# Two rates for a background conversion of weights, and twelve products of zeros early in an attention stage

## The chip, the cores and the metric

The kernel runs on one core of a Trainium2 chip. The metric is the device time of one execution in microseconds (us). The text calls the engines PE (matrix products), DVE (vector), ACT (activations), POOL and SP, as the profile does.

## What is computed

The reference is a chain of three layers on 1792 tokens (4 batches of 448). The first is attention with sigmoid weights, 12 heads of 64:

```
scores = scale * np.matmul(q, k.transpose(0, 1, 3, 2)) - np.log(S)
attn = 1.0 / (1.0 + np.exp(-scores))
return np.matmul(attn, v)
```

The second layer gives each token to one of 8 experts. Token-expert pairs are taken in falling order of their gate product, and an expert takes 224 tokens at most; each expert is two products with a ReLU between them. The third is a feed-forward layer with a leaky ReLU (2048 hidden units), whose weights `w_in` and `w_out` come in as 64-bit floating-point numbers.

## The kernel before

**Attention.** Four heads make a unit, `n`; there are 3 units in a batch and 12 in all. A unit has 7 steps (`STEPS_OF`), so there are 84 steps, numbered `i` here, 21 to a batch. For each step `scores(i)` (L368, L371) issues four products of 64x64 and one sigmoid on ACT, which does the step's whole tile; `values(i - 2)` (L391) follows two steps later (`LATE = 2`) and adds into PSUM tiles `pav`, of which there are 3. Twice per unit DVE adds two such tiles into `xT` (L397, L400), which sets a `pav` tile free. The scores' PSUM tiles `psc` are two.

**Loads.** Six loads of `qkv` go out at the start on SP's queue: five pieces of unit 0 and then all of unit 1. The load of unit n+2 is issued during unit n.

**Warming products.** `keep_warm` (L351) issues products of a tile of zeros, 128x128 times 128x384 in bf16, into a PSUM tile that nobody reads. Fourteen of them stand ahead of the first step.

**The conversion.** `narrow` (from L404 on) is a generator that turns the 64-bit words of `w_in` (16 parts) and of 13 of the 16 blocks of `w_out` into 32-bit numbers. A part is a tile of 128x768. Its operations, in their order:

- POOL issues the load of the words (L416, L418); four tiles of words exist, and the load for part i+4 is issued after part i.
- ACT takes the absolute value of the high words (L423) for even parts; DVE does this (L437) for odd parts.
- DVE clamps (L441), DVE shifts (L443), ACT scales the low words into a tile `cl` (L445), of which there are two; DVE merges the sign (L447).
- POOL adds the two (L458), and for `w_out` it issues a store of the part before (L428).

Its first `yield` stands after the first four loads. Then an odd part has four `yield`s (after L437, L441, L445, L447) and an even part three. The add on POOL (L458) comes with the next call.

**The order.** All engines work in program order. The loop over steps (L514 on) calls `scores(i)`, `aside(i)`, `values(i - 2)`, one piece of routing work if there is one, and `aside(i)` again. `aside` (from L500) adds `PACE` to an account and calls `next(back)` once for each whole unit on it. It begins with step 9. `back` is the conversion.

**Routing work.** After a batch's last value its gate products, the choice of an expert, the comparisons of all tokens (DVE, L202 to L208, more of them with every batch) and the counts (PE, L215, L219) are put on the list `todo`, which the next batch's steps take one by one; the copies of `x` to memory (`turns`, L331 on PE, L334 on ACT) go ahead of them. The last batch's pieces come after the loop. Behind them, `for _ in back: pass` calls whatever is left of the conversion. Then L897 runs, and `settle` closes expert 0: a chain from the counts over PE (L573), DVE (L578 on), POOL (`by`, L606) and a gather to the first expert's tokens.

Of the kernel before, what the change touches and what calls it, by code (L numbers as in the profile page):

```python
# [24 lines left out]
def attention_experts_ffn(  # L25
# [55 lines left out]
    ps_m = att.enter_context(tc.tile_pool(name="ps_m", bufs=1, space=PSUM))  # L81
# [8 lines left out]
    def load(n, a=0, z=3 * QV):  # L90
        if a == 0:
            qkv_sb[n] = ld.tile([P, 3 * QV], F32, name="qkv")
        nc.sync.dma_start(qkv_sb[n][:, a:z], qkv[n // NQ, n % NQ, :, a:z])
# [225 lines left out]
    def turns(b):  # L319


        x = xT[b]

        def turn(t0):
            w = min(P, S - t0)
            xt = aw.tile([P, DM], F32, name="xt", bufs=3)
            p = ps_s.tile([P, 2, 512], F32, name="psc")
            for i in range(HP):
                for s in range(w // D):
                    for z in range(2):  # L330
                        nc.tensor.matmul(p[halves[s], z, i * D:(i + 1) * D],  # L331
                                             x[halves[z], i, t0 + s * D:t0 + (s + 1) * D],
                                             ident[halves[z], halves[z]], start=True, stop=True)
            nc.scalar.copy(xt[:w].rearrange("p (i z d) -> p z i d", z=2, d=D),  # L334
                           p[:w, :, :HP * D].rearrange("p z (i d) -> p z i d", d=D))
            nc.sync.dma_start(x_dram[b * S + t0:b * S + t0 + w, :], xt[:w])

        return [lambda t0=t0: turn(t0) for t0 in range(0, S, P)]
# [7 lines left out]
    def keep_warm(ps, tag, n):  # L346
        if not n:
            return
        p = ps.tile([P, 512], F32, name=tag)[:, :3 * P]
        for _ in range(n):  # L350
            nc.tensor.matmul(p, idle[:, :P], idle, start=True, stop=True)  # L351
# [4 lines left out]
    STEPS_OF = [(0, c) for c in range(KC)] + [(None, KC)] + [(1, c) for c in range(KC)]  # L356
    steps = [(n, r, c) for n in range(B * NQ) for r, c in STEPS_OF]
    LATE = 2
    halves = [slice(0, D), slice(D, P)]

    def scores(i):
        n, r, c = steps[i]
        p = ps_s.tile([P, 2, 512], F32, name="psc")
        for s in range(2):
            for z in range(2):
                a = c * P + z * D if r is not None else KC * P
                w = r if r is not None else z
                nc.tensor.matmul(p[halves[z], s, :S], k_of(n, w, a, a + D)[halves[s]], q_of(n, w)[halves[s]],  # L368
                                 start=True, stop=True)
        AT[i] = aw.tile([P, 2, S], F32, name="at", bufs=LATE + 2)  # L370
        nc.scalar.activation(AT[i], p[:, :, :S], AF.Sigmoid, bias=bias, scale=1.0 / math.sqrt(D))  # L371

    def values(i):
        n, r, c = steps[i]
        b, m = divmod(n, NQ)
        if (r, c) == (0, 0):
            if m == 0:
                xT[b] = aw.tile([P, HP, S], F32, name="xT")
            PV[0, 1] = ps_v.tile([P, 512], F32, name="pav")
            PV[0, 0] = ps_v.tile([P, 512], F32, name="pav")  # L380
        if r is None:
            PV[1, 1] = ps_v.tile([P, 512], F32, name="pav")
        if (r, c) == (1, 0):
            PV[1, 0] = ps_v.tile([P, 512], F32, name="pav")
        a = AT.pop(i)
        for z in range(2):
            w = r if r is not None else z
            first = (w, z) == (1, 1) and r is None or (w, z) != (1, 1) and c == 0
            last = (w, z) == (0, 0) and r is None or (w, z) != (0, 0) and c == KC - 1
            for s in range(2):  # L390
                nc.tensor.matmul(PV[w, z][halves[s], :S], v_of(n, c, 2 * w + s if r is not None else s)[halves[z]],  # L391
                                 a[halves[z], s, :], start=first, stop=last)
        x = xT[b]
        if (r, c) == (0, KC - 1):
            nc.scalar.copy(x[:, 2 * m, :], PV[0, 1][:, :S])
        elif r is None:
            nc.vector.tensor_tensor(x[:, 2 * m, :], x[:, 2 * m, :], PV[0, 0][:, :S], op=OP.add)  # L397
        elif (r, c) == (1, KC - 1):
            nc.scalar.copy(x[:, 2 * m + 1, :], PV[1, 1][:, :S])  # L399
            nc.vector.tensor_tensor(x[:, 2 * m + 1, :], x[:, 2 * m + 1, :], PV[1, 0][:, :S], op=OP.add)  # L400
# [97 lines left out]
    owed = [0.0]  # L498

    def aside(i):  # L500

        if i > 8:
            owed[0] += PACE
            while owed[0] >= 1:
                next(back, None)
                owed[0] -= 1

    nc.sync.dma_start(wg[:, :, :E], w_gate.rearrange("(c p) e -> p c e", p=P))
    nc.sync.dma_start(al, alpha.rearrange("(c p) -> p c", p=P))
    PACE = 0.68  # L510
    keep_warm(ps_m, "pm", 14)
    NS = len(steps)
    BS = NQ * len(STEPS_OF)
    for i in range(NS + LATE):  # L514
        if i < NS:
            scores(i)
            n, at_step = divmod(i, len(STEPS_OF))

            if LATE < at_step <= LATE + 3 and n + 2 < B * NQ:
                a = (at_step - LATE - 1) * QV  # L520
                load(n + 2, a, a + QV)
        aside(i)
        k = i - LATE
        if k == NS - 1:
            final = after_batch(B - 1)
            final.pop(0)()
        if k >= 0:
            values(k)
        for turns_left in (rows_todo, todo):
            if turns_left:  # L530
                turns_left.pop(0)()
                break
        aside(i)
        if k >= 0 and k % BS == BS - 1:
            b = k // BS
            todo += after_batch(b) if b + 1 < B else final
            (rows_todo if b + 2 < B else rows_end).extend(turns(b))
# [792 lines left out]
```

## Time and profile before

| | us |
|---|---|
| median of 3 runs | 1005.82 |
| lowest and highest of these | 1005.04, 1006.96 |
| the profiled execution's own time | 1013.2 |
| its span, first to last instruction | 1011.3 |

The profile's span has 96% of busy PE. The attention stage with the routing of the first expert takes the first fifth (about 0 to 208 us); experts and feed-forward layers take the rest. A row of the timeline gives the start and the duration in us, then engine, line, operation, tile written and tiles read, shapes, how many are merged into the row, and in brackets the idle time of the engine before it and what ended it.

### The profile page before, as it was taken

What the parts mean: (1) busy time and instruction counts of PE and PEld (TensorE: products, weight loads), DVE (VectorE), ACT (ScalarE), POOL (GpSimd) and SP (SyncE); (2) the same over time, 40 slices, a digit from 0 to 9 for tenths busy, and PEclk for the clock granted to TensorE, in tenths of its full rate; (3) what the DMA queues carried; (4) which work ended last, traced back from release to release, by engine and by line L of the source; (5) the groups of instructions that cost most, each with busy time, mean ns of one, the idle gap of its engine ahead of it and who ended that gap; (6) DMA issues with size and microseconds to landing.
All of it is one profiled execution on the core that took longest, in us unless ns stands there. A gap on an engine that the chain in (4) does not pass through costs nothing.

```text
span 1011.3 us, 17392 instructions
## 1 busy us (share of the span) xinstructions
PE 968.4 (96%) x6793; PEld 792.3 (78%) x6793; DVE 665.9 (66%) x1297; ACT 523.8 (52%) x875; POOL 217.4 (21%) x300
## 2 busy tenths in 40 slices
PE   7999999889789999999999999999999999999995
PEld 3444433569788878899988898999999999999994
DVE  1669899797667797477777745777643477644342
ACT  3989777311454343466643344765343466644442
POOL 1435465122720000711000060300120111000001
PEclk8999999999989999999999999999999999999998
DMA  8687884465531121257403131861321167311101
GB/s 289 217 307 247 305 322 147 158 242 194 179 133 36 54 100 48 71 181 253 140 32 110 47 104 48 255 236 35 109 91 63 43 188 256 111 47 48 63 32 54
DMA packets 41523, 141.44 MB, mean 140 GB/s; under 512 B 9250, under 2 KB 9842, under 8 KB 41314
## 3 DMA queue, kind: packets, MB, share of 16 engines
q1 hardware_dynamic: 26210, 72.40, 21.2%
q0 software_dynamic: 15232, 67.95, 20.0%
q8 instruction: 53, 0.87, 0.4%
q14 instruction: 28, 0.23, 0.1%
HBM read 122.86 MB, written 17.46 MB: 139 GB/s over the span
## 4 chain that ended last, share of the span: by engine, by line
PE 70%; DVE 11%; ACT 7%; DMA 5%; issue 4%; POOL 2%; SPq 0%; DVEq 0%; ACTq 0%; POOLq 0%
PE pa L1162 18%; PE pz L1142 18%; PE pa L1060 15%; PE psc L368 4%; PE pav L391 4%; PE pa L954 2%; PE pa L934 2%; ACT si L985 2%; DMA wm<-in_w_dram 2%; PE pa L1142 1%; DVE t L1063 1%; POOL pk L762 1%; DMA qkv<-in_qkv_dram 1%; PE pa L1201 1%; DMA wo_dram<-ct 1%
## 5 line engine op out<-in xcount | busy, mean ns | idle before, releaser
L1162 PE MATMUL pa<-gx,so 128*128 128x448 f32 x1152 | 251.8, 368 | 0.3 <-issue 0.3
L1142 PE MATMUL pz<-y,si 128*128 128x448 f32 x1080 | 230.3, 367 | 1.2 <-ACT R L183 1.2
L1162 PEld LDWEIGHTS pa<-gx,so 128*128 128x128 f32 x1152 | 213.9, 188 | 19.8 <-issue 2.2
L1142 PEld LDWEIGHTS pz<-y,si 128*128 128x128 f32 x1080 | 202.1, 188 | 18.5 <-ACT R L183 1.7
L1145 ACT ACTIVATE gx<-pz 128x448 f32<-128x448 f32 x60 | 32.7, 545 | 244.6 <-PE pz L1142 244.6
L1147 DVE SCALAR_TENSOR_TENSOR gx<-gx,nalpha 128x448 f32<-128x448 f32 x64 | 43.7, 683 | 143.9 <-ACT gx L1146 130.2
L1100 POOL DMA_DIRECT2D wo<-wo_dram x64 | 35.5, 556 | 447.4 <-DVE so L1107 218.0
L1060 PE MATMUL pa<-y,si 128*128 128x448 f32 x336 | 112.8, 388 | 1.1 <-DVE y L1023 1.1
L1060 PE MATMUL pa<-gx,si 128*128 128x448 f32 x336 | 108.6, 380 | 0.0
L990 DVE TENSOR_TENSOR so<-wm,si 128x768 fp32r<-128x768 f32 (+1 forms) x98 | 103.9, 1063 | 2.1 <-PE pa L1162 1.1
L368 PE MATMUL psc<-qkv 64*64 64x448 f32 x672 | 100.2, 560 | 4.2 <-DMA qkv<-in_qkv_dram 2.9
L371 ACT ACTIVATE at<-psc,bias 128x896 f32<-128x896 f32 x84 | 84.7, 1019 | 37.4 <-PE psc L368 37.1
L391 PE MATMUL pav<-at,qkv 64*64 64x448 f32 x672 | 102.2, 553 | 1.4 <-ACT xT L399 1.0
L985 ACT CAST si<-wm 128x768 fp32r<-128x768 f32 (+1 forms) x98 | 89.7, 920 | 1.5 <-DMA wm<-in_w_dram 1.5
L1060 PE MATMUL pa<-y,so 128*128 128x224 f32 x336 | 82.9, 274 | 7.5 <-DVE so L990 7.4
L1060 PE MATMUL pa<-gx,so 128*128 128x224 f32 x336 | 83.3, 268 | 0.3
L1060 PEld LDWEIGHTS pa<-y,so 128*128 128x128 f32 x336 | 65.8, 196 | 11.9 <-DVE so L990 9.5
L1063 DVE TENSOR_TENSOR t<-pa,t 128x224 f32<-128x224 f32 x98 | 38.3, 391 | 53.1 <-ACT t L1062 47.7
L1060 PEld LDWEIGHTS pa<-y,si 128*128 128x128 f32 x336 | 63.1, 195 | 5.0 <-ACT si L985 1.3
L391 PEld LDWEIGHTS pav<-at,qkv 64*64 64x64 f32 x672 | 34.8, 136 | 41.0 <-issue 31.1
L1151 DVE TENSOR_TENSOR gx<-gx 128x448 fp32r<-128x448 f32 x64 | 40.0, 625 | 40.6 <-ACT gx L1150 40.6
L1060 PEld LDWEIGHTS pa<-gx,so 128*128 128x128 f32 x336 | 64.5, 192 | 2.7 <-DVE so L990 1.7
(215 smaller groups left out, 1438.6 us busy)
## 6 DMA issues: line engine op xcount, KB each, us to landing
wm<-in_w_dram SPq DMA_DIRECT2D x64, 384.0 KB, 4.0
wm<-in_w_dram SPq DMA_DIRECT2D x48, 512.0 KB, 4.9
wo<-wo_dram POOLq DMA_DIRECT2D x64, 384.0 KB
qkv<-in_qkv_dram SPq DMA_DIRECT2D x31, 448.0 KB, 5.3
words<-in_w_in_dram POOLq DMA_DIRECT2D x16, 768.0 KB
words<-in_w_out_dram POOLq DMA_DIRECT2D x13, 768.0 KB
wo_dram<-ct POOLq DMA_DIRECT2D x13, 384.0 KB
x_dram<-xt SPq DMA_DIRECT2D x12, 384.0 KB, 4.9
```

Source lines behind the costliest of these rows:

```text
L368: nc.tensor.matmul(p[halves[z], s, :S], k_of(n, w, a, a + D)[halves[s]], q_of(n, w)[halves[s]], start=True, stop=True)
L371: nc.scalar.activation(AT[i], p[:, :, :S], AF.Sigmoid, bias=bias, scale=1.0 / math.sqrt(D))
L391: nc.tensor.matmul(PV[w, z][halves[s], :S], v_of(n, c, 2 * w + s if r is not None else s)[halves[z]], a[halves[z], s, :], start=first, sto ...
L985: nc.scalar.copy(hi, w)
L990: nc.vector.tensor_tensor(lo, w, hi.bitcast(F32), op=OP.subtract)
L1060: nc.tensor.matmul(o, a[:, c, :], y, start=(c == 0 and s == 0), stop=(c == k - 1 and s == 1))
L1063: nc.vector.tensor_tensor(t, p[:, :CAP], t, op=OP.add)
L1100: nc.gpsimd.dma_start(RW[f], wo_dram[f * P:(f + 1) * P, :])
L1142: nc.tensor.matmul(z[:, :n], a[:, c, :], m[:, c, :n], start=(c == 0 and s == 0), stop=(c == HP - 1 and s == 2))
L1147: nc.vector.scalar_tensor_tensor(t, dn, nalpha[:, f:f + 1], up, op0=OP.mult, op1=OP.add)
L1151: nc.vector.tensor_tensor(gl, t, gh.bitcast(F32), op=OP.subtract)
L1162: nc.tensor.matmul(acc[d][:, :n], a[:, d * P:(d + 1) * P], m, start=(f == 0 and s == 0), stop=(f == NF - 1 and s == 2))
```

## The change

The account of `aside` grows by 0.95 per call up to step `BS + LATE` = 23 and by 0.57 from step 24 on, where it grew by 0.68 throughout. Twelve products of zeros are issued ahead of `scores(7)`, the first of the second unit (the second four heads).

```diff
     def aside(i):
 
         if i > 8:
-            owed[0] += PACE
+            owed[0] += EARLY if i <= BS + LATE else PACE
             while owed[0] >= 1:
                 next(back, None)
                 owed[0] -= 1
...
-    PACE = 0.68
+
+    EARLY, PACE = 0.95, 0.57
     keep_warm(ps_m, "pm", 14)
     NS = len(steps)
     BS = NQ * len(STEPS_OF)
     for i in range(NS + LATE):
+        if i == len(STEPS_OF):
+            keep_warm(ps_m, "pm", 12)
         if i < NS:
             scores(i)
```

## Rows read from the trace of the kernel before

**Rows 1.** Page, part 1: busy us of each engine over the whole span.
```profile
PE 968.4 (96%) x6793; PEld 792.3 (78%) x6793; DVE 665.9 (66%) x1297; ACT 523.8 (52%) x875; POOL 217.4 (21%) x300
```
**Rows 2.** Windows: stretch, busy us of PE, PEld, DVE, ACT, POOL, granted clock, DMA share, GB/s.
```profile
28.00:52.00 24.00, 23.14 (x273) 10.81 (x269) 17.94 (x22) 21.49 (x26) 11.60 (x10) 1.00 0.67 241
52.00:63.00 11.00, 10.64 (x230) 6.01 (x224) 5.11 (x8) 9.58 (x12) 4.10 (x5) 1.00 0.86 309
63.00:97.00 34.00, 34.00 (x429) 14.63 (x419) 31.16 (x47) 29.21 (x36) 16.71 (x14) 1.00 0.75 262
97.00:131.00 34.00, 33.42 (x413) 14.32 (x409) 28.35 (x48) 27.67 (x36) 16.46 (x14) 1.00 0.84 303
131.00:181.00 50.00, 46.04 (x536) 17.30 (x531) 45.62 (x67) 35.52 (x44) 28.25 (x26) 0.97 0.60 217
```
**Rows 3.** Timeline of ACT: the sigmoids of steps 7, 10 and 24 (one each step).
```profile
23.95 1.01 ACT L371 ACTIVATE at<-psc,bias 128x896 f32<-128x896 f32 x1 [0.50 <-PE psc L368]
...
28.76 1.01 ACT L371 ACTIVATE at<-psc,bias 128x896 f32<-128x896 f32 x1 [0.80 <-PE psc L368]
...
52.88 1.01 ACT L371 ACTIVATE at<-psc,bias 128x896 f32<-128x896 f32 x1
```
**Rows 4.** The start: PE's and SP's timelines, landing times of qkv (0:60), a window.
```profile
13.88 1.01 PE L368 MATMUL psc<-qkv 64*64 64x448 f32 x3 [2.90 <-DMA qkv<-in_qkv_dram]
...
0.77 2.77 SPq L93 DMA_DIRECT2D qkv<-in_qkv_dram  x6
...
DMA to landing us min/median/max: 2.6/6.6/15.5
...
10.00:20.00 10.00, 7.10 (x42) 2.54 (x41) 0.00 (x0) 2.59 (x3) 0.00 (x0) 0.66 0.98 331
```
**Rows 5.** Timeline of PE: products of zeros between the steps of expert 0's routing.
```profile
196.31 1.63 PE L351 MATMUL pa<-idle 128*128 128x384 bf16 x9
...
198.45 2.11 PE L351 MATMUL pa<-idle 128*128 128x384 bf16 x12
```
**Rows 6.** The conversion: timelines of POOL and DVE; groups by form, 28 to 52 us.
```profile
84.86 2.02 POOL L458 TENSOR_TENSOR w_in_sb<-ct,cl 128x768 int32<-128x768 int32 x1 [2.03 <-DVE ct L447]
...
84.62 0.56 DVE L437 TENSOR_SCALAR ct<-words 128x768 int32<-128x768 int32 x1
85.22 2.08 DVE L441 TENSOR_SCALAR ct<-ct 128x768 f32<-128x768 f32 x1
...
88.34 0.95 DVE L447 SCALAR_TENSOR_TENSOR ct<-words,ct 128x768 int32<-128x768 int32 x1
89.21 0.55 DVE L441 TENSOR_SCALAR ct<-ct 128x768 f32<-128x768 f32 x1
...
93.31 1.94 DVE L437 TENSOR_SCALAR ct<-words 128x768 int32<-128x768 int32 x1
...
L441 DVE TENSOR_SCALAR ct<-ct 128x768 f32<-128x768 f32 x5 | 4.8, 966 | 4.4 <-ACT ct L423 4.4
...
L437 DVE TENSOR_SCALAR ct<-words 128x768 int32<-128x768 int32 x3 | 4.0, 1322 | 0.0
```
**Rows 7.** The last batch: chain of waits, timelines of DVE and PE.
```profile
137.80 9.41 DMA wo_dram<-ct
...
147.33 1.06 DVE L437 TENSOR_SCALAR ct<-words 128x768 int32<-128x768 int32 x1 [1.31 <-DMA wo_dram<-ct]
...
148.81 0.35 PE L215 MATMUL pm<-g,OH 112*32 112x448 bf16 x1 [2.25 <-DVE g L208]
```
**Rows 8.** Behind the loop: DVE, POOL; and a small DVE operation beside a POOL add.
```profile
196.66 0.29 DVE L578 TENSOR_TENSOR tmp<-pc,OH 112x128 f32<-112x128 f32 x1 [1.85 <-PE pc L573]
...
180.53 1.09 POOL L428 DMA_DIRECT2D wo_dram<-ct x2
...
140.05 1.82 POOL L458 TENSOR_TENSOR ct<-ct,cl 128x768 int32<-128x768 int32 x1 [1.01 <-ACT at L371]
...
140.27 1.65 DVE L173 TENSOR_TENSOR a<-PK,M 112x32 f32<-112x32 f32 x1
```

## The prediction

> **What bounds the kernel now.** I read the page's totals first, then windows over the attention stage, then the timelines of the engines there. PE is busy for 96% of the span [rows 1], so whatever delays PE in this stage arrives at the end; the experts behind it only move as a block. The windows [rows 2] show three regimes. From 28 to 52 us (steps 10 to 23) PE idles 0.86 us, ACT is at 21.49 of 24 and DVE has 6 us free. From 63 to 131 PE is the bound: 34.00 of 34, then 33.42 of 34, with DVE at 31.16 and 28.35 right beneath it. From 131 to 181 (the last batch) PE idles 3.96 us and the granted clock is 0.97, while DVE is at 45.62 of 50. There PE waits for DVE: 2.25 us for a comparison whose turn came late behind a conversion that itself had waited 1.31 us for a store that took 9.41 us [rows 7]. The change thus takes conversion from where DVE is late and puts it where DVE has room; the question is whether that room is enough.
>
> **What the paces do.** Two calls a step at 0.68 from step 9 on make 20 calls by step 23, 73 by step 62 and the whole 102 in the loop (1 fetch, 15 even parts of 3, 14 odd of 4). At 0.95 and 0.57 it is 28 by step 23, 72 by step 62 and 99 by step 85. So steps 10 to 23 take 8 more calls, steps 24 to 62 nine fewer (44 for 53), the last batch about three fewer, and three calls are left for behind the loop.
>
> **A call's price on DVE.** Seven calls are an even and an odd part: two times L441, L443 and L447 and one L437, at 0.56, 0.56, 0.96 and 0.56 us [rows 6], 4.7 us. While POOL adds, though, a DVE operation takes as long as the add: L441 2.08 us instead of 0.55 beside POOL's 2.02 [rows 6]. A full DVE pays 1.5 us per part, 7.7 us per seven calls, 1.1 us a call. The stretch from 84.62 to 93.31 holds exactly seven calls and two sums of L397 and L400: 8.7 us, so 0.5 is left for each sum.
>
> The Trainium skill (SBUF — State Buffer, Who interferes with whom) says that DVE and POOL share a port pair that is locked for a whole instruction, and whoever comes second blocks fully. The trace agrees with 2.08 us beside 0.55.
>
> **Part A, the zeros.** Twelve products take (2.11 - 1.63) / 3 = 0.16 us each [rows 5], together 1.9 us of PE at full clock. They stand ahead of step 7, whose sigmoid came at 23.95 in an unbroken cadence [rows 3]. Unit 1's load was the sixth issued, by 3.54 us, and no load took over 15.5 us [rows 4]: it was there by 19.0, so step 7 waited for nothing. Steps 7 to 9 have no conversion beside them, so nothing else hides the zeros: +1.9 (0 if step 7 does wait).
>
> **Part B, the first batch.** Calls 2 to 28 put seven whole parts and most of an eighth on DVE: 27 x 4.7 / 7 = 18 us, plus seven POOL adds at 1.5 (10.5), plus four sums of some 0.5 (2): 30.5 us. The room is from 30.6 us (the first absolute value on ACT behind step 10's sigmoid at 28.76) to step 24's scores, a us ahead of 52.88 [rows 3]: some 21.5 us. DVE is then 9 us late. PE feels that in two places: ACT's L445 has two tiles `cl` and waits for the POOL add of two parts earlier, and that wait holds the sigmoids behind it; and the sums free the `pav` tiles. Five calls lie between an add and the L445 that needs its tile, worth 5.5 us of DVE less the add's own 1.8; two steps between scores and values and three to four between a sum and its tile's next use cover 2 to 5 us more. So 9 us late is 1 to 5 us on PE. From below: the five adds in this stretch lengthened DVE by only 5 x 0.41 + 3 x 0.77 = 4.3 us [rows 6], 0.87 each; then DVE is 4.6 late, all of it covered, and what is left is ACT: 8 calls with 3 operations in seven, each at most the 1.01 us of a sigmoid, which is on a larger tile [rows 3], are up to 3.4 us against its 2.5 us of idle time [rows 2]; I put +0.5 there. I take +2.0 (0.5 to 5.5), nearer the lower row because the lengthening is seen in this very stretch. From 52 to 63 DVE has 5.9 us free and PE is held by the copies of x, so DVE's delay ends there. The words' loads move on too: 8 calls are 2.3 parts of 768 KB, in 24 us 75 GB/s on 241; the window of [rows 4] carried 331, so I cost this at nothing.
>
> **Part C, steps 28 to 62.** Nine calls fewer are 10 us less on DVE, but PE has only 0.58 us of idle time to give back [rows 2]: -0.5 (0 to -0.6).
>
> **Part D, the last batch.** The ceiling is PE's idle 3.96 us and the clock, 0.03 x 50 = 1.5 us: -5.5. DVE arrives without the backlog of the second and third batch and does three calls fewer, 3.3 us; the store has 3.1 steps per part where it had 2.6, so its wait of 1.31 us goes, and with it the idle time ahead of the lower clock. DVE is then at 45.62 - 3.3 = 42.3 us beside PE's 50 - 5.5 = 44.5, near enough that some waits stay: -4.5 (-2.5 to -5.5).
>
> **Part E, behind the loop.** L458 of one part and the whole last part come after the comparisons. On DVE 0.56 + 0.56 + 0.96 = 2.1 us go ahead of L578, where DVE idles for 1.85 us [rows 8]: +0.2. Then POOL's add of 1.8 us meets the short operations of `settle`; one of 112x32 elements took 1.65 us beside such an add [rows 8]. POOL also issues two stores ahead of `by` and the gather, 1.09 us for two. Everything up to the first expert waits for this chain. Bounds: +0.2 (the add falls into a wait for PE) and +3.1 (0.2, 1.8 and 1.1 in full); I take +1.5.
>
> **Sum.** 1.9 + 2.0 - 0.5 - 4.5 + 1.5 = +0.4 us on the profiled execution's 1013.2. That execution is 7.4 us above the median of 1005.82; I carry the difference over: 1006.2. About 0.2% (2 us) is what a measurement of this kernel can tell from no change.
>
> **The rivals.**
> 1. *The room suffices.* DVE's lengthening stays at the 0.87 us of the old first batch, the backlog is gone from step 28 on, and the last batch reaches its ceiling: 1.9 + 0.5 - 0.6 - 5.5 + 0.2 = -3.5, 1002.3; lower where idle time that the modelled ends of PE's products hide comes back as well. For it: DVE's 6 us free. Against it: 27 calls ask for more than that.
> 2. *The zeros fill a wait.* If unit 1's load came after step 6, PE would idle there and its clock fall, as after the 2.90 us at 13.88: the stretch from 10 to 20 us was granted 0.66, part of it the lower of the two levels (1.2 GHz for 2.4) [rows 4], 3.4 of 10 us lost. Then A is not +1.9 but up to -3.4: 1000.9. Against it: the landing by 19.0. The Trainium skill (TensorE: Matmul & The Clock Gate, HAM oscillation — how this bites in real kernels) says that a PE left idle in waits for loads is throttled again and each burst starts cold, for which zeros would be the cure. By that rule the first wait is such a place and the trace agrees (0.66); the zeros stand behind it.
> 3. *The first batch becomes DVE's* (slower). Every add lengthens DVE by 1.5 us, and the two `cl` tiles pass the delay on to the sigmoids. A step then asks DVE for 1.9 x 1.1 + 0.15 = 2.2 us in the 1.7 that a step took there (24.1 us for 14 [rows 3]), so from step 18 on DVE is over 4 us late, and that decides it. Then B is 5.5, the last batch gives 2.5 and the tail costs 3.1: 1.9 + 5.5 - 2.5 + 3.1 = +8.0, 1013.8; with the tail at 1.5 it is +6.4. For it: the full lengthening in the row at 85.22. Against it: this stretch's mean of 0.87.
>
> By the lock rule of the SBUF page taken alone every add would block a full DVE, which is rival 3.
>
> **Chances.** Forecast 0.36 (0.28 within the bound, 0.03 faster, 0.05 slower), rival 1 0.30 (all faster), rival 2 0.07 (0.05 faster, 0.02 within), rival 3 0.27 (slower). Faster 0.38, same 0.30, slower 0.32. The forecast's own range is 1004 to 1008.5; the range over all, 1000 to 1011, leaves out the far ends of rivals 2 and 3.
>
> **What would show it.** A: twelve L351 near 23 us, step 7's sigmoid 1.9 later, with no wait for qkv. B: L441 or L437 near 2 us at most adds before step 24, waits of L445 for POOL, PE idle over 0.86 us there. C and D: PE idle in the last batch under 2 us, clock 1.00. E: L458 beside L578 to L596 and `settle` longer by 1 to 2 us. If PE shows no idle time before step 24, B is wrong; if the last batch still idles by 4 us, D is.

## The result and the profile after

The changed kernel takes **1014.58 us** (median of 4 runs, 1012.85 to 1021.71) where the kernel before took 1005.81 beside it: a ratio of 1.0102, with a 95% interval of 1.006 to 1.0143. That is 8.8 us slower, and above the range of the prediction. The profiled execution is the longest of the four, 1021.71 us with a span of 1019.8.

The engine totals hardly differ. First the page's totals of the changed kernel, which answer to [rows 1]:

```profile
PE 973.5 (95%) x6805; PEld 793.8 (78%) x6805; DVE 666.1 (65%) x1297; ACT 523.4 (51%) x875; POOL 221.7 (22%) x300
```

DVE's instructions are the same 1297, PE's are twelve more. So the time is in when things happen. The start of the same event in both profiled executions, stage by stage (the sigmoids are those of ACT's timeline, as in [rows 3]; the others are the first transposes of the last counts on PE, L573 of before, and the first products of experts and of the feed-forward layer):

| stretch | before, us | after, us | difference |
|---|---|---|---|
| sigmoid of step 6 to that of step 7 | 1.5 | 3.7 | +2.2 |
| steps 10 to 24 | 24.1 | 30.1 | +6.0 |
| steps 24 to 83 | 122.8 | 115.4 | -7.4 |
| step 83 to the transposes L573 | 20.1 | 27.0 | +6.9 |
| the transposes to `tmp` (L578) | 0.8 | 6.9 | +6.0 |
| `tmp` to the first product of expert 0 | 15.1 | 15.5 | +0.4 |
| that product to the feed-forward layer's first | 95.6 | 87.9 | -7.7 |
| from there to the end | 703.9 | 706.4 | +2.5 |

Step 83's sigmoid stands at 175.7 us before and at 176.1 after: within the loop, cost and gain cancel. The loss stands behind the loop. The last two rows are stages that the change does not touch; the row of 95.6 and 87.9 lies between 86.7 and 100.8 over all profiled executions below, so I judge the change by what comes ahead of it. The 95.6 also belongs to an execution of the kernel before that took 7.4 us more than its median. How late step 6 comes differs as well (19.2 to 22.8 us over the executions), so I compare stretches rather than positions.

The windows of the changed kernel, with the columns of [rows 2] (busy us of PE, PEld, DVE, ACT and POOL, granted clock, DMA share, GB/s), cut at its own stages:

```profile
30.00:61.00 31.00, 26.41 (x282) 10.21 (x278) 27.95 (x30) 25.50 (x32) 17.54 (x14) 0.97 0.68 237
...
133.00:176.00 43.00, 42.29 (x447) 16.52 (x441) 37.54 (x60) 34.84 (x43) 21.47 (x22) 1.00 0.70 252
176.00:203.00 27.00, 23.49 (x451) 14.97 (x443) 18.20 (x37) 10.60 (x16) 4.67 (x4) 0.75 0.40 148
203.00:225.50 22.50, 15.03 (x100) 9.73 (x99) 14.60 (x49) 3.33 (x8) 8.61 (x13) 0.85 0.41 133
```

In the first batch DVE is at 27.95 of 31 and PE idles for 4.6 us, where it idled for 0.86 [rows 2]. In the last batch PE idles for 0.71 us in 43 at full clock, where it was 3.96 in 50 at 0.97 [rows 2]. From 203 to 225.5 PE is idle for a third of the time.

**The zeros** stand where they were expected. ACT's sigmoids of steps 6 and 7 of the changed kernel, to hold against [rows 3]:

```profile
22.13 1.01 ACT L371 ACTIVATE at<-psc,bias 128x896 f32<-128x896 f32 x1 [0.49 <-PE psc L368]
25.87 1.01 ACT L371 ACTIVATE at<-psc,bias 128x896 f32<-128x896 f32 x1 [2.73 <-PE psc L368]
```

**The first batch.** The next rows are from the timelines of POOL, DVE, PE and ACT after, and the last two group DVE's operations by form from 30 to 60 us (busy us, mean ns of one):

```profile
34.84 2.01 POOL L458 TENSOR_TENSOR w_in_sb<-ct,cl 128x768 int32<-128x768 int32 x1 [30.68 <-DVE ct L447]
...
39.42 1.98 POOL L458 TENSOR_TENSOR w_in_sb<-ct,cl 128x768 int32<-128x768 int32 x1 [2.02 <-DVE ct L447]
...
35.19 2.08 DVE L441 TENSOR_SCALAR ct<-ct 128x768 f32<-128x768 f32 x1
...
39.77 2.05 DVE L443 TENSOR_SCALAR ct<-ct 128x768 int32<-128x768 int32 x1
...
43.73 1.65 DVE L441 TENSOR_SCALAR ct<-ct 128x768 f32<-128x768 f32 x1
...
47.47 2.06 DVE L443 TENSOR_SCALAR ct<-ct 128x768 int32<-128x768 int32 x1
...
55.19 2.06 DVE L443 TENSOR_SCALAR ct<-ct 128x768 int32<-128x768 int32 x1
...
58.16 0.61 DVE L400 TENSOR_TENSOR xT<-xT,pav 128x448 f32<-128x448 f32 x1
...
53.09 0.98 PE L368 MATMUL psc<-qkv 64*64 64x448 f32 x8 [1.47 <-ACT at L371]
...
58.83 0.34 PE L331 MATMUL psc<-ident,xT 64*64 64x64 f32 x8 [2.06 <-DVE xT L400]
...
44.99 0.94 ACT L445 ACTIVATE cl<-words 128x768 int32<-128x768 uint32 x1 [0.42 <-POOL w_in_sb L458]
...
51.23 0.90 ACT L423 ACTIVATE ct<-words 128x768 f32<-128x768 f32 x1 [1.14 <-DMA words<-in_w_in_dram]
...
L443 DVE TENSOR_SCALAR ct<-ct 128x768 int32<-128x768 int32 x7 | 8.4, 1200 | 0.2
L441 DVE TENSOR_SCALAR ct<-ct 128x768 f32<-128x768 f32 x7 | 7.6, 1086 | 3.1 <-ACT ct L423 3.1
```

Every add of POOL now finds DVE with something queued and lengthens one operation from 0.55 us to between 1.65 and 2.08; L441 and L443 have means of 1086 and 1200 ns where an undisturbed one takes 0.56 [rows 6]. DVE runs late, and PE feels it at 58.83: the copies of `x` (L331) wait 2.06 us for the sum of L400, which DVE reached only at 58.16.

The wait of 1.47 us at 53.09 comes from further back: ACT had stood 1.14 us for a load of words at 51.23, which POOL issues only after an add. That load is not the limit. In the eight profiled executions, this one and seven of the experiments, that have this first batch with full adds, PE idles 4.57 to 4.59 us between steps 10 and 24 and the stretch takes 30.0 to 30.2 us, also in those three in which ACT waits 0.12 us or less for words. What they share is DVE, busy for 27.95 of 31 us in the window above. After the pauses the clock was granted 0.68 from 58 to 61 us, where before had 1.00 [rows 2].

**Behind the loop.** Timelines of DVE and POOL after, answering to [rows 8], then what the view of the tile `ct` says from 198 us on (who waited for it, and its stores from issue to landing):

```profile
201.91 0.55 DVE L441 TENSOR_SCALAR ct<-ct 128x768 f32<-128x768 f32 x1
...
203.97 0.17 DVE L900 TENSOR_SCALAR nalpha<-al 128x16 f32<-128x16 f32 x1
209.97 0.29 DVE L581 TENSOR_TENSOR tmp<-pc,OH 112x128 f32<-112x128 f32 x1 [5.83 <-issue]
...
204.20 1.79 POOL L458 TENSOR_TENSOR ct<-ct,cl 128x768 int32<-128x768 int32 x1 [17.82 <-ACT cl L445]
205.95 1.09 POOL L428 DMA_DIRECT2D wo_dram<-ct  x2
...
  DVE tmp L581: 5.8, 1
...
DMA to landing us min/median/max: 2.6/2.9/3.2
```

`tmp`, the first operation of `settle` on DVE, reads `pc` and `OH` alone, and PE's transposes into `pc` start at 203.10; before, it followed them by 0.8 us, here by 6.9, at 209.97. The profile's "issue" names no releaser, but the second of the last two stores goes out at 206.5 and 3.2 us later it has landed: 209.7, 0.27 us ahead of `tmp`. Before, the wait there was 1.85 us for PE, and the last two stores had been issued at 180.53 [rows 8].

### The profile page after: what moved, and what is told of

The parts are those of the page before. It is cut to its first block, busy times and chain, and to the rows that moved or that the text cites. A ratio compares the mean times of both kernels' runs of the same rounds, so it can differ in the third digit from the quotient of the medians.

```text
span 1019.8 us, 17409 instructions
## 1 busy us (share of the span) xinstructions
PE 973.5 (95%) x6805; PEld 793.8 (78%) x6805; DVE 666.1 (65%) x1297; ACT 523.4 (51%) x875; POOL 221.7 (22%) x300
## 3 DMA queue, kind: packets, MB, share of 16 engines
q1 hardware_dynamic: 26210, 72.40, 21.5%
## 4 chain that ended last, share of the span: by engine, by line
PE 63%; DVE 15%; issue 6%; ACT 6%; DMA 5%; POOL 4%; SPq 0%; DVEq 0%; POOLq 0%; ACTq 0%
PE pa L1165 18%; PE pz L1145 18%; PE pa L1063 13%; POOL pk L765 3%; PE psc L368 3%; PE pav L391 3%; PE pa L937 2%; DMA wm<-in_w_dram 2%; DVE ct L443 1%; PE pa L1145 1%; ACT si L988 1%; DMA qkv<-in_qkv_dram 1%; DVE t L1066 1%; DVE g L208 1%; PE pa L1204 1%
## 5 line engine op out<-in xcount | busy, mean ns | idle before, releaser
L1150 DVE SCALAR_TENSOR_TENSOR gx<-gx,nalpha 128x448 f32<-128x448 f32 x64 | 43.7, 684 | 145.1 <-ACT gx L1149 145.1
L371 ACT ACTIVATE at<-psc,bias 128x896 f32<-128x896 f32 x84 | 84.4, 1012 | 36.6 <-PE psc L368 35.9
L368 PE MATMUL psc<-qkv 64*64 64x448 f32 x672 | 91.9, 561 | 5.8 <-DMA qkv<-in_qkv_dram 3.3
L391 PE MATMUL pav<-at,qkv 64*64 64x448 f32 x672 | 93.3, 548 | 0.9 <-ACT xT L399 0.8
L1063 PEld LDWEIGHTS pa<-gx,si 128*128 128x128 f32 x336 | 61.3, 189 | 4.4 <-DVE gx L1071 0.6
```

The costliest lines, as they stand in the source:

```text
L1063: nc.tensor.matmul(o, a[:, c, :], y, start=(c == 0 and s == 0), stop=(c == k - 1 and s == 1))
L1150: nc.vector.scalar_tensor_tensor(t, dn, nalpha[:, f:f + 1], up, op0=OP.mult, op1=OP.add)
```

## The experiments

Two accounts were to be told apart. **The tail**: the three calls left behind the loop cost most of the loss, because `settle` waits for the last stores. **The first batch**: its 6 us are the loss (rival 3 of the prediction), and the tail is small. The first four experiments shared one chip, on which before had a median of 1005.06 us (1001.78 to 1006.65). On the chips of the later ones before lay at 1013.48 and 1012.53, with runs up to 15 and 17 us apart, so there the stages of the profiles say more than the ratios.

**Without the zeros.** From the changed kernel:

```diff
-        if i == len(STEPS_OF):
-            keep_warm(ps_m, "pm", 12)
```

> The changed kernel without its twelve products of zeros. Theory 1 (the three calls left behind the loop cost most: settle's first vector operation waits for the last stores): about 1.9 us under the changed kernel, 1012.7 against 1014.6, since the zeros are plain PE time ahead of step 7. Theory 2 (the denser first batch costs most): the same 1.9. If the zeros save a clock drop, this run is no faster or slower than the changed kernel.

Measured: 1014.31 us, 1.0097 (1.007 to 1.0125). The paces carry the loss, with the zeros or without. The 1.9 us that both accounts expected back do not show in the median, which is 0.3 us lower. Steps 10 to 24 take 30.2 us, and `tmp` comes 6.9 us after the transposes, as in the changed kernel.

**All calls done in the loop.** From the changed kernel, zeros kept:

```diff
-    EARLY, PACE = 0.95, 0.57
+    EARLY, PACE = 0.95, 0.61
```

> The changed kernel with 0.61 for 0.57, so that all 102 calls and the last add come inside the loop, as before the change; 0.95 and the zeros stay. Theory 1: 6 to 9 us under the changed kernel (1006 to 1008.5), and settle's first vector operation starts within 0.5 us of the transposes it reads. Theory 2: no change, 1013 to 1015, as the first batch is the same.

Measured: 1009.63 us, 1.0046 (1.003 to 1.0062), 5.0 us less than the changed kernel's median where I had expected 6 to 9. The first batch is as long as there (30.2 us), so it is not what made the difference. In the timelines of DVE and POOL of this kernel the last stores leave at 185.20, ahead of the end, and `tmp` waits for PE again, as before:

```profile
201.35 0.29 DVE L581 TENSOR_TENSOR tmp<-pc,OH 112x128 f32<-112x128 f32 x1 [1.85 <-PE pc L576]
...
185.20 1.09 POOL L428 DMA_DIRECT2D wo_dram<-ct  x2
```

**The tail alone.** From the kernel before, one pace that also leaves three calls behind the loop:

```diff
-    PACE = 0.68
+    PACE = 0.645
```

> The kernel before with one pace of 0.645 for 0.68: 99 calls in the loop, three left, no dense first batch, no zeros. Theory 1: 5 to 8 us over the kernel before (1011 to 1014), with a wait of about 6 us at settle's first vector operation. Theory 2: within 1 us of the kernel before, 1005 to 1007.

Measured: 1013.22 us, 1.0076 (1.0046 to 1.0106), 8.2 us above before's median. Steps 10 to 24 keep their length (24.2 us) and steps 10 to 83 even take 141.9 where before took 146.9. All that and more is lost behind the loop: 47.8 us from step 83 to the first expert's product, where before took 36.0. Timelines of DVE and POOL there, then PE's wait for DVE behind step 83 and a window (columns as above), and last that wait in the kernel before:

```profile
195.46 0.17 DVE L897 TENSOR_SCALAR nalpha<-al 128x16 f32<-128x16 f32 x1
201.47 0.29 DVE L578 TENSOR_TENSOR tmp<-pc,OH 112x128 f32<-112x128 f32 x1 [5.84 <-issue]
...
197.43 1.09 POOL L428 DMA_DIRECT2D wo_dram<-ct  x2
...
175.09 0.77 PE L256 MATMUL pm<-ident,l 128*112 128x128 f32 x2 [3.59 <-DVE l L254]
...
175.00:180.00 5.00, 4.91 (x106) 3.59 (x106) 1.53 (x3) 2.08 (x3) 0.17 (x1) 0.50 0.19 73
```

```profile
178.86 0.47 PE L256 MATMUL pm<-ident,l 128*112 128x128 f32 x2 [0.92 <-DVE l L254]
```

The second store goes out at 198.0 and lands 3.2 us later, at 201.2; `tmp` follows at 201.47. Of the 11.8 us lost, 6.0 are this wait. Another 5.2 lie between step 83 and the transposes: PE waits 3.59 us for DVE where it had waited 0.92, and then runs at half the clock.

This is the run that decides: a kernel without the busy first batch and without zeros has the loss, and one with both but without the calls behind the loop has half of it, most of which the zeros cost by themselves (next run).

**The zeros alone.** From the kernel before:

```diff
+        if i == len(STEPS_OF):
+            keep_warm(ps_m, "pm", 12)
```

> The kernel before with the twelve products of zeros ahead of step 7 and nothing else. Both theories: 1.9 us over the kernel before, 1007.7, with step 7's sigmoid 1.9 us later. If something later hides them: 1005.8.

Measured: 1008.57 us, 1.0036 (1.0025 to 1.0048), 3.5 us slower. The sigmoids of steps 6 and 7 are 3.7 us apart, as after, so 2.2 us are in place; where the other 1.3 us arise this profile does not settle (steps 10 to 83 take 1.6 us less than in the profile of before, and the way from there to the first expert 1.0 more). The costs do not add up: without the zeros the changed kernel lost as much as with them.

**Stores ahead of the last part.** From the changed kernel: the last two stores are issued with the one before them and from its tile, which leaves two blocks of `w_out` with another block's values; the calls and the last add stay.

```diff
-                _, f, h = parts[i]
-                nc.gpsimd.dma_start(wo_dram[...], outs.pop(i).bitcast(F32))
+                t = outs.pop(i).bitcast(F32)
+                if i < len(parts) - 2:
+                    for _, f, h in parts[i:] if i == len(parts) - 3 else parts[i:i + 1]:
+                        nc.gpsimd.dma_start(wo_dram[...], t)
```

> The changed kernel, with the last two stores of converted weights issued together with the one before them and from its tile (two blocks of 128 rows of w_out are wrong), so that no store follows the last add; the add and the vector operations stay where they are. Theory 1: settle's first vector operation starts at the end of the last add, about 3.8 us earlier: 1010 to 1011.5. If the wait is for the add and not for the stores: no gain, 1014.

Measured: 1017.0 us, 1.0015 (0.9966 to 1.0064), with runs from 1008.76 to 1025.22, so the stage has to tell. The transposes and `tmp` are 2.9 us apart where the changed kernel has 6.9. Timelines of DVE and POOL:

```profile
198.98 0.29 DVE L583 TENSOR_TENSOR tmp<-pc,OH 112x128 f32<-112x128 f32 x1 [1.89 <-POOL ct L460]
...
197.14 1.80 POOL L460 TENSOR_TENSOR ct<-ct,cl 128x768 int32<-128x768 int32 x1 [12.56 <-ACT cl L447]
```

With the stores out of the way `tmp` waits for the next thing in line, the end of POOL's add on `ct` at 198.94, although it does not read `ct`. So here the wait is for the last user of `ct`, a store or an add, and not for the stores as such. In the code `att.close()` stands between L897 and `settle`; that the tiles behind it take over the space, and so wait for all that still uses the old ones, is the reading that fits, and no run tested it by itself.

**The rest of the conversion ahead of the last batch's pieces.** From the changed kernel, and again from the kernel before with 0.645 in place of 0.68:

```diff
+    for _ in back:
+        pass
     for _ in range(2):
         rows_end.pop(0)()
```

> The changed kernel, with the three calls that are left drained right behind the loop, ahead of the last batch's routing pieces instead of behind them. Theory 1 (settle's first vector operation waits for the last stores): that wait of 5.8 us falls to what it was before the change, 1.85 us behind the transposes; the calls' 2 to 4 us of vector time move ahead of the comparisons; 3 to 6 us under the changed kernel, 1009 to 1012. Theory 2 (the first batch): no gain, 1013 to 1016.

> The kernel before with one pace of 0.645 and the three calls left drained right behind the loop. In the run with 0.645 alone step 83 came 6.5 us earlier than before and the wait behind the loop took 6. Theory 1: the wait goes, the gain in the loop stays in part: 1001 to 1005, at or under the kernel before. Theory 2 (the conversion must be early to be cheap): 1006 to 1009.

> The changed kernel with the three calls that are left drained right behind the loop, measured again because the first session's times scattered. Theory 1: 0 to 6 us under the changed kernel of this call; from step 83 to the first expert's product some 43 us, without a wait between the transposes and settle's first vector operation. Theory 2: as the changed kernel.

Measured: 1026.97 (three runs above 1026 and one at 1011.33), 1023.46 (1.0102, 1.0032 to 1.0172) and, the first again, 1027.19 (1.0132, 1.0067 to 1.0197). The wait ahead of `tmp` is gone in all three (0.8 us after the transposes), but the pieces wait behind the calls instead: step 83 to the transposes takes 28.2, 30.7 and 27.5 us where before needs 20.1, so from step 83 to the first expert it is 43.7, 46.7 and 43.5. The clock was granted half (1.2 GHz for 2.4) for some 10 us in that stretch or more each time, from 185.3 to 195.5 in the first. That this costs the gain is a miss of mine. On top, the stage from the first expert to the feed-forward layer took 100.2 to 100.8 us in these three. ACT's timeline of the first shows two pauses in it:

```profile
282.09 0.34 ACT L1067 COPY t<-pa 128x224 f32<-128x224 f32 x1 [4.95 <-remote]
...
290.62 0.34 ACT L1067 COPY t<-pa 128x224 f32<-128x224 f32 x1 [6.62 <-remote]
```

"remote" is a releaser that the profile cannot name. No edit touches that stage, and the last experiment has the same 100.7 us without this edit. Eleven of the twelve runs of these kernels lie above 1020 us, so the long stage is no rare chance with them, and their ratios do not say what draining first costs by itself. What causes the pauses stays open.

**The two paces without either cost.** From the changed kernel, no zeros and 0.61:

```diff
-    EARLY, PACE = 0.95, 0.57
+    EARLY, PACE = 0.95, 0.61
...
-        if i == len(STEPS_OF):
-            keep_warm(ps_m, "pm", 12)
```

> The changed kernel without zeros and with 0.61 for 0.57, all calls in the loop: what the two paces alone do. The first batch (steps 10 to 24) should take 6 us more than before, 30 us for 24, and steps 24 to 83 some 5 to 6 us less. Theory 1: within 2 us of the kernel before, 1004 to 1007.5. Theory 2: 1008 to 1011.

Measured: 1010.85 us, 0.9985 (0.9941 to 1.0029): the same as before. Steps 10 to 24 take 30.2 us (+6.1), steps 24 to 83 117.1 (-5.7), the way from step 83 to the first expert 36.6 (before 36.0). The busy first batch alone costs nothing at the end, since the steps behind it give it back.

**The changed kernel again, beside one with less to convert.** The second is the kernel before with 12 blocks of `w_out` in place of 13 in this generator (the other four are converted later) and a pace at which all is done in the loop:

```diff
-    FA = 13
+    FA = 12
...
-    PACE = 0.68
+    PACE = 0.655
```

> The changed kernel once more, beside the others of this call: 7 to 10 us over the kernel before. Step 83 within 2 us of before, and from there to the first expert's first product 43 to 50 us where before took 36.

> The kernel before with 12 blocks of w_out converted in the loop for 13 (the other four then come beside the experts) and one pace of 0.655, at which all calls fit into the loop. Theory 1: step 83 some 4 us earlier, as at 0.645, no wait behind the loop, 36 us to the first expert as before: 1001 to 1004 where before has 1005. If the block costs as much beside the experts as it saves: 1005 to 1007.

Measured: the changed kernel 1017.53 us, 1.0065 (1.0014 to 1.0116), 5.0 us over before where I had expected 7 to 10; with twelve blocks 1012.96, 1.0024 (0.999 to 1.0058), no gain. There steps 10 to 83 take 145.3 us for 146.9, not 4 us less, and the way to the first expert is 36.4. The profile of the first tells more. Steps 10 to 83 take 145.3 us (145.4 in the first profile of this kernel), and `tmp` comes 6.9 us after the transposes. But step 83 to the transposes takes 21.5 us there, not 27.0. Two rows of PE's timeline, the changed kernel first and then this second execution, and a window of each with the columns above:

```profile
180.42 0.47 PE L256 MATMUL pm<-ident,l 128*112 128x128 f32 x2 [1.84 <-DVE l L254]
...
182.00:195.50 13.50, 12.90 (x223) 9.00 (x214) 7.13 (x20) 5.36 (x8) 2.31 (x2) 0.50 0.37 134
```

```profile
177.44 0.47 PE L256 MATMUL pm<-ident,l 128*112 128x128 f32 x2 [1.81 <-DVE l L254]
...
176.00:195.00 19.00, 15.67 (x398) 10.28 (x399) 16.37 (x36) 9.00 (x13) 2.44 (x3) 1.00 0.52 189
```

The same wait for DVE, 1.84 and 1.81 us, was followed by 13.5 us at a granted clock of 0.50 in one execution and by 1.00 in the other. Of the changed kernel's 49.3 us from step 83 to the first expert (before 36.0), 5.5 are this; the second execution has 43.5. Yet the fall keeps to one kind of kernel. Between step 83 and the transposes the clock fell in seven of the nine profiled executions with calls left behind the loop, and in none of the five (before among them) with all calls in it. The wait ahead of it was 1.81 to 3.59 us in the seven, 1.81 and 1.83 in the two that kept the clock, and 0.92 to 2.12 in the five. That the left calls bring the fall on is thus likely, and not shown.

**Short adds.** From the changed kernel, POOL's adds of the first eight parts cut to 8 of every 128 columns; DVE writes that half of `w_in` with zeros once, so most of it stays zero:

```diff
+            if i < 8:
+                o, t, r = o[:, :, :8], t[:, :, :8], r[:, :, :8]
             nc.gpsimd.tensor_tensor(o, t, r, op=OP.add)
...
+    nc.vector.memset(w_in_sb[:, :, :8 * P], 0.0)
```

> The changed kernel with POOL's adds (L458 of the kernel before) of the first eight parts cut to 8 of every 128 columns, so that they take a fraction of 1.8 us; the calls, their DVE and ACT operations and the loads of words stay. This leaves most of the first half of w_in as zeros, which DVE writes once at the start. Steps 10 to 24 took 24.1 us before and 30.1 after. Theory (the adds lengthen DVE's operations by 1.1 to 1.5 us each, DVE falls behind, its late sums hold the turns of x and the scores): 18 us of calls and 2 of sums fit the stretch, steps 10 to 24 fall back to 24 to 26 us, and L441 and L443 stay near 0.55 and 0.95 us there. Rival (the eight calls more are too much by themselves, through ACT's share of them or the words' loads, whatever the adds do): 29 to 30 us. Step 83 by the theory 4 to 6 us earlier than the 173 to 176 of the changed kernel's executions, unless the later steps take it back; what comes behind the loop stays as in the changed kernel, with the wait of 5.8 us ahead of the first operation of settle.

Measured: one run, 1023.14 us beside one of 1017.45 for before. Steps 10 to 24 take 25.9 us, where the changed kernel takes 30.1 and before 24.1. Groups of DVE by form from 30 to 60 us, and a window from 30 to 53:

```profile
L441 DVE TENSOR_SCALAR ct<-ct 128x768 f32<-128x768 f32 x9 | 5.1, 568 | 6.7 <-ACT ct L423 6.7
L443 DVE TENSOR_SCALAR ct<-ct 128x768 int32<-128x768 int32 x9 | 5.0, 559 | 0.3
...
30.00:53.00 23.00, 22.18 (x220) 8.88 (x214) 18.00 (x28) 23.00 (x29) 6.56 (x14) 1.00 0.82 305
```

The theory holds: with short adds L441 and L443 are back at 0.56 us and 4.2 of the 6.0 us are gone. Short adds also let the loads of words go out earlier, but by the eight executions named above those did not set the time. What stays is 1.8 us; with ACT busy for 23.00 of 23.00 us I put it down to ACT, which no run tested by itself. Steps 10 to 83 take 140.3 us, and behind the loop `tmp` again follows the transposes by 6.9 us. That the time is long all the same is the stage of 100.7 us told above.

## Why the prediction was wrong

The prediction said 1006.2, and its rival 3 said 1013.8. The measured 1014.58 is next to rival 3, but not for its reason alone.

- **What the paces do** was right: the conversion's calls fell as counted, and one add with the whole last part came behind the loop (L441 at 201.91 is the last part's first operation).
- **Part A** (+1.9) was right to 0.3 us: +2.2 in place (the row of [rows 5] for twelve products, 2.11 us as a whole, was nearer than the 1.9 from its slope). Rival 2, that the zeros fill a wait, falls: step 7 moved by all of it. Alone the zeros cost 3.5 us of time (2.5 to 4.8).
- **Part B** (+2.0, 0.5 to 5.5) was mis-sized: +6.0. The lengthening was taken at the 0.87 us per add of the old first batch; it was 1.1 to 1.5 us, close to what rival 3 had, because DVE now has an operation at hand whenever POOL adds. Short adds took 4.2 us of it away. The Trainium skill (SBUF — State Buffer, Who interferes with whom) says that a DVE instruction in a two-port mode and one of POOL share a port pair, and that whichever comes second is blocked for the other's whole instruction; the trace agrees, with 2.08 us beside an add and 0.56 without. Two paths carried it that Part B did not list or undercounted. The copies of `x` wait for DVE's last sum (2.06 us at 58.83), where I had let the delay end in them. And ACT's share of the eight calls is, by the run with short adds, up to 1.8 us, not 0.5. The path that both Part B and rival 3 put first, L445 waiting for POOL's add over the two `cl` tiles, came to 0.42 us here and to 1.3 us in all at most in the other executions. So rival 3 had the size of B from the right lengthening, but in part by the wrong path. The loads of words, costed at nothing, held ACT for 1.14 us, though without them the batch was as long.
- **Part C** (-0.5, at most -0.6) was too small. Sigmoid 24 to sigmoid 63 takes 79.8 us before (52.88 to 132.66) and 76.8 after (60.76 to 137.51): -3.0. I had put the ceiling at PE's idle time of 0.58 us. The idle time in this stretch fell only from 0.94 to 0.60 us, the busy time by 2.7, so a busy PE there was not a PE at its peak.
- **Part D** (-4.5) held: step 63 to step 83 takes 43.0 us before and 38.6 after, -4.4, with the store's wait and the lower clock gone.
- **Part E** (+1.5, 0.2 to 3.1) is the step that failed. It priced the calls behind the loop by their DVE operations, by POOL's add beside short operations and by POOL's time to issue two stores ahead of `by`. The price was another: `settle`'s first operation waits for those stores to land and for the add to end, 5.8 us in the timeline, +6.0 against before. Besides, the transposes come later after step 83 than before: by 1.4 us in the second execution (21.5 to 20.1), which a kernel without calls behind the loop shows too (21.4 with the zeros alone), and by 5.5 more in the first, where the clock fell. From step 83 to the first expert that is +7.5 (43.5 to 36.0) to +13.3 (49.3 to 36.0). With all calls in the loop it was 36.4 to 37.0 in four kernels.

With the terms as the second execution has them (A, B, C and D together, the way behind step 83), the sum up to the first expert is 2.2 + 6.0 - 7.5 + 7.5 = +8.2 us, beside the 8.8 measured. Rival 3's +8.0 came from A 1.9, B 5.5, D -2.5 and E 3.1: B was near, the C of -3.0 was missing, D was too small by 2 and E too small by 4. That its total came out is luck: its deciding point, the first batch, is given back by the later steps, as the two paces without the tail show (0.9985). Rival 1 fell with Part B.

The fault in Part E was visible: the prediction costed a store at its issue, and asked who waits for POOL's queue, but not who waits for the landing. The rows of before could not show that wait, since its last stores were issued 15 us earlier, and I set no row for it as an upper bound. The landing of a store of this tile in the last batch, 9.41 us [rows 7], was the row to take.

No version beat the kernel before: the two paces with all calls in the loop and without the zeros are equal to it within 0.6%, and twelve blocks as well.

## What to carry to other kernels

When background work is spread over a loop, finish it inside the loop. Here what was left over met the point where the stage's tiles are given up, and the first vector operation behind that point waited for the last store to land, though it reads none of its data; that the memory changing hands is the reason is my reading. Price a leftover transfer by its landing, not by its issue, and look for the first instruction behind the close of a pool. And when you move work of two engines that hinder each other to a place with room, take the full hindrance as the price, since the room was what kept it low.

## What was not expected of the hardware

- A DVE operation of 112x128 elements that reads neither waited 5.8 us for two stores and, with these away, 1.89 us for an add of POOL on the same stage's tile.
- The same wait of PE, 1.84 and 1.81 us, led to 13.5 us at half the clock in one execution and to none in another of the same kernel; over all profiled executions such a fall stood only in kernels with calls left behind the loop, in seven of nine.
- On one chip the kernel before stayed within 5 us of itself, on two others it spread over 15 to 17 us; four of the profiled executions, all on these or a third, have two pauses each of 3.6 to 8 us that the profile calls "remote", in a stage that no edit touched. Whether these make the spread is open.
